# Warm-up matmuls on a constant, two more groups of them in the first step, and four score matmuls in another order

## The chip, the cores and the metric

The kernel runs on one core of one Trainium2 chip. The metric is device time of one execution in microseconds (us), as a median over runs. Less is better.

## What is computed

The reference chains three parts, all in float32:

```python
# attention: 2 batches x 8 heads, 768 tokens, head size 64
q_bucket = sum(((q @ proj) > 0) * 2**arange(6))     # six sign bits per query, the same for keys
mask     = q_bucket[..., :, None] == k_bucket[..., None, :]
scores   = where(mask, (q @ k.T) / sqrt(64), -1e9)
attn     = softmax(scores) @ v
x        = attn as (1536 tokens, 512)
# two feed-forward layers, 512 -> 2048 -> 512
h = x @ w_in;  g = h * sigmoid(1.702 * h);    x = g @ w_out
h = x @ w_in;  g = h * tanh(softplus(h));     out = g @ w_out
```

## The kernel before, in words

The kernel gets float32 precision out of float32r matmuls (one reduced-precision product each) by splitting operands into a high and a low part and adding three products. It has two stages: attention (about the first 226 us) and the feed-forward layers.

Attention is a pipeline of 96 steps, 16 heads with 6 blocks of 128 queries each. The order of every engine's instructions is written out by hand in the loop over `i` at the end of `attention` (the string `ORDER` and the table `todo`); the scheduler changes nothing, and each engine works through its own list in that order. In a step, `qk` (L512 to L526) computes one block of 128 x 768 scores in two PSUM halves of 384 columns: two matmuls of `qx` with `kh` (the scaled dot products) and then two of `qb` with `kb`, the sign bits and the rest of the split operands, which add the mask. Below, these second two are "the mask rows". `clamp` (L528, VectorE) takes the row minimum, `expo` (L537, ScalarE) the exponential, `trp` (L577) transposes on TensorE, `trl` (VectorE) makes the low part, and `pv` (L597) multiplies with the values. The score tile `s` has two buffers, so the scores of step 2 wait until the clamp of step 0 has read its tile.

Ahead of the loop stands what this change touches. `ident`, a 128 x 128 identity, is made on GpSimd, and TensorE then runs `NWARM` = 24 transposes of it into a PSUM tile nobody reads (L365 to L367). Meanwhile the first head's operands arrive and are prepared in `first` (L454 to L483): `qk_m`, `kh` and `qx` on VectorE and ScalarE, a copy into `qb` and one into `kb` on GpSimd (`pcopy`, L91), six matmuls `logits` (L425, tiles `pt`) for the sign bits, a comparison on VectorE (L479) that writes the bits into `qb`, and a copy of them into `kb` on ScalarE (L483). After that `qk(0)` is called once, and the loop calls `qk(1)` in its first step:

```python
            qk(0)
            for i in range(NSTEP + PVLAG):
...
                    elif op == "Q" and i + 1 < NSTEP:
                        qk(i + 1)
```

Of the kernel before, what the change touches and what calls it, by code (L numbers as in the profile page):

```python
# [12 lines left out]
F32 = mybir.dt.float32  # L13
# [27 lines left out]
def lsh_attention_moe_kernel(  # L41
# [10 lines left out]
    nc = tc.nc  # L52
    B, H, D, S = qt.shape
    NTOK, DM = out.shape
    P = 128
# [13 lines left out]
    NWARM = 24  # L69
# [222 lines left out]
    def r_in(m, f, k0=0, k1=KD):  # L292
        if k0 == 0:
            pool, tag = mps["h"], f"h{f % 2}"
            if (m, f // 2) == (0, 1):
                pool, tag = (mps["q"], "Y") if f % 2 else (mps["h"], "y0")
            h_t[m, f] = pool.tile([P, CH], F32, tag=tag, name="h")
        h = h_t[m, f]
        wh, wl = w_t[m, f, 0]
        n = 3 * k0  # L300
        for kk in range(k0, k1):
            wk = slice(kk * P, (kk + 1) * P)
            for a, x in ((wh, xr_hi), (wh, xr_lo), (wl, xr_hi)):
                nc.tensor.matmul(  # L304
                    h, a[:, wk], x[:, kk], start=(n == 0), stop=(n == 3 * KD - 1)
                )
                n += 1

    def attention():
        with ExitStack() as es:  # L310
# [7 lines left out]
            ps_t = es.enter_context(tc.tile_pool(name="ps_t", bufs=3, space=PSUM))  # L318
            ps_u = es.enter_context(tc.tile_pool(name="ps_u", bufs=1, space=PSUM))
            es_s = ExitStack()  # L320
            ps_s = es_s.enter_context(tc.tile_pool(name="ps_s", bufs=2, space=PSUM, side="right"))
# [40 lines left out]

            ident = cst.tile([P, P], F32, name="ident")
            make_identity(nc, ident)
            warm = ps_t.tile([P, 512], F32, tag="pt", name="warm")  # L365
            for _ in range(NWARM):
                nc.tensor.transpose(warm[:, :P], ident, ident)  # L367
            zero = pp.tile([P, 2, HS], F32, tag="p", name="zero").rearrange("p a b -> p (a b)")
            nc.vector.memset(zero[32:64], 0.0)
            qb_tiles = [cst.tile([P, S], F32R, name=f"qb{i}") for i in range(2)]  # L370
# [132 lines left out]
            st_t = {}  # L503
# [5 lines left out]
            rb_t = {}  # L509
            scr = dr.tile([NHD, S], F32, name="scr")  # L510

            def qk(i):  # L512
                n, t = divmod(i, NT)
                kh, qx, qb, kb, _ = opnd[n]
                s = ps_s.tile([P, 2, 512], F32, tag="s", name="s")
                c = slice(t * P, (t + 1) * P)
                for a, bb, st in ((qx, kh, True), (qb, kb, False)):
                    for f in range(2):
                        nc.tensor.matmul(  # L519
                            s[:, f, :HS],  # L520
                            a[:, c],
                            bb[:, f * HS : (f + 1) * HS],
                            start=st,
                            stop=not st,
                        )
                st_t[i] = s  # L526

            def clamp(i):  # L528
                s = st_t[i]
                sb = pp.tile([P, 2, HS], F32, tag="p", name="p")  # L530
                mn = sm.tile([P, 1], F32, tag="mn", name="mn")
                nc.vector.tensor_scalar(  # L532
                    sb, s[:, :, :HS], NEG, None, ALU.min, ALU.min, accum_out=mn
                )
                st_t[i] = (sb, mn)

            def expo(i):  # L537
                sb, mn = st_t.pop(i)
                n, t = divmod(i, NT)
                p = sb.rearrange("p a b -> p (a b)")  # L540
                if t == 0:
                    z_t[n] = sm.tile([P, NT], F32, tag="z", name="z", bufs=3)
                nc.scalar.activation(  # L543
                    p,
                    p,
                    AF.Exp,
                    bias=mn,
                    scale=-1.0,
                    accum_out=z_t[n][:, t : t + 1],
                )  # L550
                p_t[i] = p
# [25 lines left out]
            def trp(g, t):  # L577
                ptile = ps_t.tile([P, 512], F32, tag="pt", name="pt")
                for j in range(3):
                    nc.tensor.transpose(  # L580
                        ptile[:, j * P : (j + 1) * P],
                        p_t[3 * g + j][:, t * P : (t + 1) * P],
                        ident,
                    )
                hi = ptp.tile([P, HS], F32R, tag="pth", name="pth")
                lo = ptp.tile([P, HS], F32R, tag="ptl", name="ptl")
                nc.scalar.copy(hi, ptile[:, :HS])  # L587
                pt_t[g, t] = (hi, lo, ptile)

            def trl(g, t):  # L590
                hi, lo, ptile = pt_t[g, t]
                nc.vector.tensor_sub(lo, ptile[:, :HS], rnd(hi))  # L592
                if t == NT - 1:
                    for j in range(3):
                        p_t.pop(3 * g + j)

            def pv(g, t):  # L597
                n, f = divmod(g, 2)
                hi, lo, _ = pt_t.pop((g, t))
                if t == 0:  # L600
                    u_t[g] = ps_u.tile([P, 512], F32, tag="u", name="u")
                ut = u_t[g]
                vv = opnd[n][4][0]
                nc.tensor.matmul(ut[:, :HS], vv[:, t, :], hi, start=(t == 0), stop=False)  # L604
                nc.tensor.matmul(ut[:, :HS], vv[:, t, :], lo, start=False, stop=(t == NT - 1))  # L605
                if t == NT - 1:
                    u_out(g)
# [93 lines left out]
            for k in range(2):  # L701
                st = NSTEP - 4 * NT * (2 - k)
# [15 lines left out]
            for n, g in enumerate((ssums, ssums, ssums, ssums, ssplit, ssplit)):  # L718
                at(NSTEP - 12 + n, sgo, g, 0, 0)

            qk(0)
            for i in range(NSTEP + PVLAG):
                if i == NSTEP:
                    es_s.close()
                    mps["h"] = ctx.enter_context(
                        tc.tile_pool(name="ps_h", bufs=1, space=PSUM, side="right")
                    )
                parts = iter(range(max(0, 2 * (i - NSTEP)), min(2 * (i - NSTEP) + 2, 2 * KD)))
                for part in parts:
                    r_in(0, part // KD, part % KD, part % KD + 1)  # L730
                    break
                kk = i - LAG
                tr = 0 <= kk < NSTEP
                g, j = divmod(kk, 3)
                kv = i - PVLAG
                gv, jv = divmod(kv, 3)
                for op in ORDER:
                    if op == "A" and tr:
                        trp(g, 2 * j)
                    elif op == "B" and tr:  # L740
                        trp(g, 2 * j + 1)
                    elif op == "a" and tr:
                        trl(g, 2 * j)
                    elif op == "b" and tr:
                        trl(g, 2 * j + 1)
                    elif op == "C" and i < NSTEP:
                        clamp(i)
                    elif op == "E" and i < NSTEP:
                        expo(i)
                    elif op == "Q" and i + 1 < NSTEP:  # L750
                        qk(i + 1)
                    elif op == "P" and 0 <= kv < NSTEP:
                        pv(gv, 2 * jv)
                    elif op == "R" and 0 <= kv < NSTEP:
                        pv(gv, 2 * jv + 1)
                    elif op == "T":
                        while todo and min(todo) <= i:
                            st = min(todo)
                            f, args = todo[st].pop(0)
                            if not todo[st]:  # L760
                                del todo[st]
                            f(*args)
                for part in parts:
                    r_in(0, part // KD, part % KD, part % KD + 1)
# [5 lines left out]
    def moe():  # L770
        with ExitStack() as es:
# [266 lines left out]
            while due:  # L1038
                flush()

    attention()
    moe()

# [58 lines left out]
```

## Time and profile before

| | |
|---|---|
| median of 3 runs | 737.72 us (737.62 to 738.42) |
| the profiled execution's own time | 737.77 us |
| its span, first to last instruction | 736.0 us |
| TensorE busy | 728.4 us, 99% of the span |
| VectorE, ScalarE, GpSimd busy | 602.1, 423.8 and 186.0 us |

The rows come from one profiled execution. Times count from the start of its span. PE is TensorE's matmul, PEld its weight load, DVE VectorE, ACT ScalarE, POOL GpSimd, SP SyncE, and L12 is line 12 of the kernel. Matmuls are pipelined, so a matmul's own duration is longer than the distance from it to the next one. A releaser, after the arrow, is what ended an engine's idle time.

### The profile page before, as it was taken

The numbers are of one execution on the slowest core, as the hardware profiler recorded it, in microseconds if no ns is written. First come the engines' busy times: TensorE is split into PE (matmuls) and PEld (weight loads), VectorE is DVE, ScalarE is ACT, GpSimd is POOL, SyncE is SP. The second block draws the span as 40 slices with busy tenths as digits, with TensorE's granted clock in tenths as the row PEclk, the third lists the DMA queues.
The fourth block names the chain that finished last, engine by engine and source line by source line (L and its number), as shares of the span: only waits on it lengthen the run. The fifth ranks groups of instructions, "written<-read, shape, count | busy, mean of one in ns | idle before, by whom it ended". The sixth has DMA issues, their size and how long they took to land.

```text
span 736.0 us, 10689 instructions
## 1 busy us (share of the span) xinstructions
PE 728.4 (99%) x3694; PEld 631.8 (86%) x3694; DVE 602.1 (82%) x1100; ACT 423.8 (58%) x846; POOL 186.0 (25%) x190
## 2 busy tenths in 40 slices
PE   8999999999999999999999999999999999999997
PEld 7999999999998788888888888888888888888886
DVE  8888889989988958786687897997598797978854
ACT  7888888888888756426153461574555254352420
POOL 8868877887893000000000000000000000000000
PEclk9999999999999999999999999999999999999999
DMA  6665565566524312031221331101131211311004
GB/s 163 164 153 151 158 176 152 158 174 163 170 73 132 95 57 86 29 114 35 80 75 41 114 116 58 57 1 57 58 115 35 80 60 55 109 35 58 1 0 172
DMA packets 26054, 69.59 MB, mean 95 GB/s; under 512 B 4464, under 2 KB 6992, under 8 KB 26000
## 3 DMA queue, kind: packets, MB, share of 16 engines
q1 hardware_dynamic: 25712, 68.81, 31.5%
q8 instruction: 29, 0.48, 0.3%
q14 instruction: 25, 0.20, 0.1%
q10 hardware_dynamic: 288, 0.10, 0.1%
HBM read 49.19 MB, written 3.19 MB: 71 GB/s over the span
## 4 chain that ended last, share of the span: by engine, by line
PE 94%; ACT 3%; DMA 1%; DVE 1%; issue 1%; POOL 0%; ACTq 0%; POOLq 0%
PE y L835 36%; PE h L304 12%; PE X L889 9%; PE s L519 8%; PE pt L580 8%; PE Y L889 6%; PE W L889 6%; PE u L605 4%; PE u L604 4%; PE prep L425 2%; ACT p L543 2%; ACT pth L587 1%; DMA qn<-in_qt_dram 0%; DMA ul<-uh 0%; DVE p L532 0%
## 5 line engine op out<-in xcount | busy, mean ns | idle before, releaser
L592 DVE TENSOR_TENSOR ptl<-pt,pth 128x384 fp32r<-128x384 f32 x192 | 98.2, 553 | 25.3 <-ACT pth L587 24.6
L587 ACT CAST pth<-pt 128x384 fp32r<-128x384 f32 x192 | 83.0, 484 | 30.2 <-PE pt L580 30.0
L217 ACT CAST wh<-wb 128x512 fp32r<-128x512 f32 x64 | 39.7, 621 | 105.0 <-DVE wb L201 53.4
L849 DVE TENSOR_TENSOR xq<-xq,y 128x512 f32<-128x512 f32 (+1 forms) x113 | 76.6, 680 | 21.9 <-PE y L835 20.8
L543 ACT ACTIVATE p<-p,mn 128x768 f32<-128x768 f32 x96 | 91.1, 949 | 1.6 <-DVE p L532 1.5
L532 DVE TENSOR_SCALAR_CACHE_REDUCE p<-s 128x768 f32<-128x768 f32 x96 | 90.5, 944 | 0.4 <-PE s L519 0.4
L580 PE MATMUL pt<-ident,p 128*128 128x128 f32 x576 | 80.9, 274 | 0.6 <-ACT p L543 0.3
L835 PE MATMUL y<-wl,gh 128*128 128x512 f32 (+1 forms) x194 | 75.1, 387 | 0.0
L835 PE MATMUL y<-wh,gl 128*128 128x512 f32 (+1 forms) x194 | 75.1, 387 | 0.0
L835 PE MATMUL y<-wh,gh 128*128 128x512 f32 (+1 forms) x194 | 75.1, 387 | 0.0
L835 PE MATMUL y<-gh,wh 128*128 128x512 f32 x192 | 74.9, 390 | 0.0
L835 PE MATMUL y<-gl,wh 128*128 128x512 f32 x192 | 74.7, 389 | 0.0
L835 PE MATMUL y<-gh,wl 128*128 128x512 f32 x192 | 74.7, 389 | 0.0
L580 PEld LDWEIGHTS pt<-ident,p 128*128 128x128 f32 x576 | 68.3, 140 | 7.3 <-ACT p L543 2.0
L604 PE MATMUL u<-pth,vv 128*128 128x384 f32 x192 | 64.9, 338 | 0.0
L605 PE MATMUL u<-ptl,vv 128*128 128x384 f32 x192 | 64.8, 337 | 0.0
L519 PE MATMUL s<-kh,qx 128*128 128x384 f32 x192 | 55.4, 369 | 0.4 <-DVE p L532 0.4
L519 PE MATMUL s<-kb,qb 128*128 128x384 f32 x192 | 50.0, 340 | 0.6 <-POOL kb L91 0.5
L304 PE MATMUL h<-xr_hi,wh 128*128 128x512 f32 x128 | 50.0, 390 | 0.0
L304 PE MATMUL h<-xr_hi,wl 128*128 128x512 f32 x128 | 49.8, 389 | 0.0
L304 PE MATMUL h<-xr_lo,wh 128*128 128x512 f32 x128 | 49.8, 389 | 0.0
L219 DVE TENSOR_TENSOR wl<-wb,wh 128x512 fp32r<-128x512 f32 x62 | 42.5, 687 | 5.5 <-ACT wh L217 4.6
(202 smaller groups left out, 1678.1 us busy)
## 6 DMA issues: line engine op xcount, KB each, us to landing
raw<-in_wt_dram SPq DMA_DIRECT2D x64, 512.0 KB
kn<-in_kt_dram SPq DMA_DIRECT2D x15, 384.0 KB
qn<-in_qt_dram SPq DMA_DIRECT2D x16, 192.0 KB
vn<-in_vt_dram SPq DMA_DIRECT2D x8, 384.0 KB
ul<-uh SPq DMA_DIRECT2D x16, 192.0 KB
rb<-scr SPq DMA_DIRECT2D x16, 192.0 KB
qx<-qk_m SPq DMA_DIRECT2D x15, 192.0 KB
qb<-qk_m SPq DMA_DIRECT2D x15, 192.0 KB
```

The lines of the kernel that those rows point to most:

```text
L304: nc.tensor.matmul(h, a[:, wk], x[:, kk], start=(n == 0), stop=(n == 3 * KD - 1))
L519: nc.tensor.matmul(s[:, f, :HS], a[:, c], bb[:, f * HS : (f + 1) * HS], start=st, stop=not st,)
L532: nc.vector.tensor_scalar(sb, s[:, :, :HS], NEG, None, ALU.min, ALU.min, accum_out=mn)
L543: nc.scalar.activation(p, p, AF.Exp, bias=mn, scale=-1.0, accum_out=z_t[n][:, t : t + 1],)
L580: nc.tensor.transpose(ptile[:, j * P : (j + 1) * P], p_t[3 * g + j][:, t * P : (t + 1) * P], ident,)
L587: nc.scalar.copy(hi, ptile[:, :HS])
L592: nc.vector.tensor_sub(lo, ptile[:, :HS], rnd(hi))
L604: nc.tensor.matmul(ut[:, :HS], vv[:, t, :], hi, start=(t == 0), stop=False)
L605: nc.tensor.matmul(ut[:, :HS], vv[:, t, :], lo, start=False, stop=(t == NT - 1))
L835: nc.tensor.matmul(y, w[:, js] if m == 0 else x[:, js], x if m == 0 else w[:, i0:i1], start=(n == 0), stop=(n == 5),)
L849: nc.vector.tensor_add(acc, acc, y)
L889: nc.tensor.matmul(bk[b], w[:, k], x, start=(first and n == 0), stop=(hook is not None and n == 2), skip_group_check=True,)
```

## The change

The 24 warm-up instructions become plain float32 matmuls of a constant tile of ones (128 x 128 stationary, 64 moving columns) in place of transposes of `ident`. The same helper is called twice more, with 3 and with 6 matmuls. `qk` can now issue its two halves apart, and the first two matmuls of step 1 are issued ahead of the mask rows of step 0.

```diff
-            warm = ps_t.tile([P, 512], F32, tag="pt", name="warm")
-            for _ in range(NWARM):
-                nc.tensor.transpose(warm[:, :P], ident, ident)
+            ones = nc.const_aps.tensor(1.0, [P, P], F32)
+
+            def keep_warm(n):
+                t = ps_t.tile([P, 512], F32, tag="pt", name="warm")
+                for _ in range(n):
+                    nc.tensor.matmul(t[:, :64], ones, ones[:, :64], start=True, stop=True)
+
+            keep_warm(NWARM)
...
-            def qk(i):
+            def qk(i, parts=(0, 1)):
                 n, t = divmod(i, NT)
                 kh, qx, qb, kb, _ = opnd[n]
-                s = ps_s.tile([P, 2, 512], F32, tag="s", name="s")
+                if 0 in parts:
+                    st_t[i] = ps_s.tile([P, 2, 512], F32, tag="s", name="s")
+                s = st_t[i]
                 c = slice(t * P, (t + 1) * P)
-                for a, bb, st in ((qx, kh, True), (qb, kb, False)):
+                both = (qx, kh, True), (qb, kb, False)
+                for a, bb, st in [both[x] for x in parts]:
...
-            qk(0)
+            qk(0, (0,))
+            qk(1, (0,))
+            keep_warm(3)
+            qk(0, (1,))
...
-                        qk(i + 1)
+                        qk(i + 1, (0, 1) if i else (1,))
+                        if i == 0:
+                            keep_warm(6)
```

TensorE is the only engine whose list changes. Its list before, from the warm-up to the scores of step 2 (`s_208`, `s_222` and `s_236` are the score tiles of steps 0, 1 and 2):

```order
L367 MATMUL warm_128<-ident_123 128x128 x24
L425 MATMUL pt_193<-qk_m_170,pwt_164 128x384
...
L425 MATMUL pt_197<-qx_169,pwt_164 128x384
L519 MATMUL s_208<-kh_168,qx_169 128x384 x2
L519 MATMUL s_208<-kb0_157,qb0_155 128x384 x2
L519 MATMUL s_222<-kh_168,qx_169 128x384 x2
L519 MATMUL s_222<-kb0_157,qb0_155 128x384 x2
L519 MATMUL s_236<-kh_168,qx_169 128x384 x2
```

The same stretch of TensorE's list in the change (the score tiles of steps 0, 1 and 2 are `s_208`, `s_211` and `s_247` there, and the line numbers are those of the changed kernel):

```order
L372 MATMUL warm_128<-const-float32-1.0 128x64 x24
L432 MATMUL pt_193<-qk_m_170,pwt_164 128x384
...
L432 MATMUL pt_197<-qx_169,pwt_164 128x384
L529 MATMUL s_208<-kh_168,qx_169 128x384 x2
L529 MATMUL s_211<-kh_168,qx_169 128x384 x2
L372 MATMUL warm_214<-const-float32-1.0 128x64 x3
L529 MATMUL s_208<-kb0_157,qb0_155 128x384 x2
L529 MATMUL s_211<-kb0_157,qb0_155 128x384 x2
L372 MATMUL warm_231<-const-float32-1.0 128x64 x6
L529 MATMUL s_247<-kh_168,qx_169 128x384 x2
```

Between the two groups of `s_208` now stand the first two matmuls of step 1 and three warm-ups; six more warm-ups stand between step 1 and step 2. The lists of VectorE, ScalarE, GpSimd and SyncE hold the same instructions in the same order as before.

## Rows read from the trace of the kernel before

**Rows 1.** The page's parts 1 and 4: busy time by engine, and the chain that ended last.
```profile
PE 728.4 (99%) x3694; PEld 631.8 (86%) x3694; DVE 602.1 (82%) x1100; ACT 423.8 (58%) x846; POOL 186.0 (25%) x190
...
PE 94%; ACT 3%; DMA 1%; DVE 1%; issue 1%; POOL 0%; ACTq 0%; POOLq 0%
```

**Rows 2.** Busy time by stretch; after the engines the granted clock, DMA share and GB/s.
```profile
0.00:7.40 7.40, 6.02 (x26) 5.65 (x27) 5.59 (x8) 5.48 (x10) 4.57 (x12) 1.00 0.69 195
7.40:14.00 6.60, 5.68 (x30) 4.67 (x28) 5.61 (x11) 3.92 (x8) 6.30 (x6) 1.00 0.70 173
14.00:16.00 2.00, 1.86 (x15) 1.60 (x14) 1.76 (x4) 1.58 (x5) 1.83 (x3) 1.00 0.32 74
16.00:20.00 4.00, 4.00 (x28) 3.71 (x26) 4.00 (x10) 4.00 (x10) 3.83 (x4) 1.00 0.71 167
30.00:60.00 30.00, 30.00 (x203) 29.24 (x202) 26.48 (x59) 25.49 (x61) 20.56 (x21) 1.00 0.60 152
```

**Rows 3.** The chain of waits from 0 to 17 us, in order of time.
```profile
8.36 0.84 POOL kb L91
...
9.25 0.45 PE s L519
9.69 0.03 issue
9.73 0.46 PE s L519
10.19 0.02 issue
10.21 0.98 DVE p L532 x2
11.19 0.04 issue
11.23 0.98 PE s L519 x4
12.21 0.02 issue
12.23 0.98 DVE p L532 x2
```

**Rows 4.** Timeline, 0 to 20 us: start us, us, what, count, idle before.
```profile
0.95 0.70 DVE L369 MEMSET zero<- 32x768 f32 x1 [0.95 <-PEq L1082]
...
7.88 1.25 DVE L479 TENSOR_SCALAR qb<-pt,mc 64x384 fp32r<-64x384 f32 x2 [0.79 <-PE pt L425]
...
8.58 1.10 ACT L483 CAST kb<-qb 32x384 fp32r<-32x384 f32 x2 [1.00 <-DVE qb L479]
...
10.36 0.52 PE L519 MATMUL s<-kb,qb 128*128 128x384 f32 x2
...
11.10 0.95 DVE L532 TENSOR_SCALAR_CACHE_REDUCE p<-s 128x768 f32<-128x768 f32 x1
```

**Rows 5.** The tile of the warm-up: min/median/max ns, first and last start.
```profile
L367 PEld LDWEIGHTS warm<-ident x24: 183/230/230, 1.4 to 6.1; 128*128 128x128 f32 x24
L367 PE MATMUL warm<-ident x24: 421/421/476, 1.4 to 6.3; 128*128 128x128 f32 x24
```

**Rows 6.** TensorE's timeline in the steady pipeline.
```profile
35.59 0.82 PE L580 MATMUL pt<-ident,p 128*128 128x128 f32 x6
```

**Rows 7.** Groups by shape: count, then busy us, mean ns, idle before and its releasers.
```profile
L580 PE MATMUL pt<-ident,p 128*128 128x128 f32 x576 | 80.9, 274 | 0.6 <-ACT p L543 0.3
```

**Rows 8.** TensorE's timeline: start us, us, what, count, idle before and its releaser.
```profile
1.36 5.38 PE L367 MATMUL warm<-ident 128*128 128x128 f32 x24 [1.36 <-POOL ident masks.py:199]
6.76 0.66 PE L425 MATMUL pt<-qk_m,pwt 128*128 128x384 f32 x1
7.22 0.44 PE L425 MATMUL pt<-kh,pwt 128*128 128x384 f32 x1
7.50 0.33 PE L425 MATMUL pt<-qx,pwt 128*128 128x384 f32 x1
7.68 0.33 PE L425 MATMUL pt<-qk_m,pwt 128*128 128x384 f32 x1
...
8.20 0.51 PE L519 MATMUL s<-kh,qx 128*128 128x384 f32 x2
```

**Rows 9.** Line L465, which writes the operand of the first `logits` matmul.
```profile
L465 DVE TENSOR_TENSOR qk_m<-kn,kh x2: 542/806/1071, 5.5 to 6.5; 64x384 fp32r<-64x384 f32 x2
```

**Rows 10.** Weight loads by shape: two products with the same weights, in a later stage.
```profile
L835 PEld LDWEIGHTS y<-wh,gl 128*128 128x128 f32 x194 | 36.4, 188 | 7.4
...
L835 PEld LDWEIGHTS y<-wh,gh 128*128 128x128 f32 x194 | 36.4, 188 | 7.4
```

**Rows 11.** TensorE's waits for weights, 0 to 30 us: engine, line, releaser, total, times, longest.
```profile
PEld s L519 <- POOL kb L91: 0.9, 1, 0.9
PEld s L519 <- DVE p L532: 0.7, 1, 0.7
```

More of the change, by code (lines that the diff above doesn't have):

```diff
@@ L525, in qk @@
                         )
-                st_t[i] = s
             def clamp(i):
```

## The prediction, as made before the changed kernel was run

> **What bounds the kernel now.** I read the page first, then the busy time by stretch, then the timeline and the chain of the first 17 us, because the change touches nothing later. TensorE is busy 99% of the span and carries 94% of the chain that ended last [rows 1]. From 16 us on there is no room left: it is busy 4.00 of 4.00 us, and later 30.00 of 30.00 [rows 2]. So whatever the start gains or loses is carried to the end unchanged, and the forecast is one sum: by how much the scores of step 2 move, which are the last thing that still waits in the start.
>
> In the first 14 us TensorE is not yet the bound. The chain there reads [rows 3]: GpSimd's copy into `kb` ends at 9.20, the mask rows of step 0 start at 9.25 (first half) and 9.73 (second half), the clamp of step 0 at 10.21, the scores of step 2 at 11.23 once that clamp has given the tile back, the clamp of step 2 at 12.23. The second half waits for ScalarE's copies into `kb` (8.58, 1.10 us for two), and these for VectorE's comparison at 7.88, and that for the `logits` matmuls [rows 4].
>
> **The clock.** The granted-clock column shows 1.00 from the first stretch on [rows 2], but the durations say otherwise, and I go by them. The 24 transposes start from 1.4 to 6.3 us, 4.9/23 = 0.213 us apart [rows 5]. The same instruction later comes every (0.82 - 0.27)/5 = 0.11 us (six in 0.82, of which the last one's duration is 0.27) [rows 6, 7]. 128 columns loaded and 128 streamed, one after the other, are 256 columns: 0.213 us at 1.2 GHz, 0.107 at 2.4. So the warm-up runs at the low level throughout. The first `logits` matmul takes 0.66 us, the second 0.44, all from 7.50 on 0.33 [rows 8]: the clock rose between 7.2 and 7.5, say 7.44, 6.1 us after TensorE began at 1.36.
>
> **Removed: the wait for `ident`.** TensorE waited until 1.36 for GpSimd's identity [rows 8]. VectorE, free of that, starts at 0.95 [rows 4], and so will the warm-up: 0.41 us earlier. By itself this is worth nothing, because the first `logits` matmul is not held by the warm-up. Its operand comes from VectorE's L465, which starts at 5.5 and takes 1.07, so ends at 6.6 [rows 9], and the matmul starts at 6.76. It can bring a clock that rises earlier. With the clock up, the three `logits` of the first half lie 0.17 us apart, as at 7.50 and 7.68, and the last starts at 7.10 rather than 7.50 [rows 8]: up to 0.35 us for the chain. There it stops, since GpSimd's 9.20 then ends last.
>
> **Added: 24 float32 matmuls of 64 columns for 24 transposes.** No such instruction is in the trace. All others here are float32r or transposes, so its price is the unknown of this forecast. Bounds from the nearest rows, at the low clock: below, one load of 128 and one stream of 64 columns, 192 columns or 0.16 us; above, four products (high and low of both operands), each with its own load, 4 x 192 = 768 columns or 0.64 us. That loads aren't shared is what a later stage shows: L835 multiplies with `wh` twice, and each of the two products has its 194 loads [rows 10]. I take the middle: two loads (a high and a low stationary operand) and four streams, 512 columns, 0.427 us at the low and 0.213 at the full clock. It is nearest to the transposes' row, at twice its price. The Trainium skill, "TensorE: Matmul & The Clock Gate", section "Terms", says that the transpose mode is 4 times faster for FP32. By that page a plain matmul of half as many columns would cost two transposes, an estimate of 0.427 us too; no run yet shows it.
>
> The sum: TensorE starts at 0.95 and the clock rises 6.1 us later, at about 7.03. By then 6.08/0.427 = 14.2 are done, and the other 9.8 take 9.8 x 0.213 = 2.1 us. The warm-up ends at 9.1, and the first `logits` starts there instead of 6.76. The warm-up has become a wait. From there the old distances hold, at the full clock: the third `logits` ends 0.68 after the first starts and VectorE begins 0.04 later; from its start at 7.88 to the second half of the mask rows at 9.73 it was 1.85 us [rows 3, 4]. So the mask rows' second half is at 9.1 + 0.72 + 1.85 = 11.7, against 9.73.
>
> **Moved: two matmuls of step 1, and 3 warm-ups.** On TensorE's own list, six `logits` and four score matmuls at 0.175 (7.50 to 8.20 is four of them [rows 8]) and three warm-ups at 0.213 put the first half of the mask rows at 9.1 + 1.75 + 0.64 = 11.5 and the second at 11.65. This lies just beside the chain's 11.7, so it costs nothing here. The move itself gains nothing: step 1's mask rows were done by 10.88, and VectorE came to that tile at 11.10, straight from the clamp of step 0 [rows 4].
>
> **Added: 6 warm-ups ahead of step 2.** TensorE's wait for the first clamp had 0.7 us [rows 11]. Counted from the second half of the mask rows, the scores of step 2 came 11.23 - 9.73 = 1.50 us later. Now three more matmuls (0.52) and six warm-ups (1.28) must pass: 1.80. That is 0.30 over the old wait. At 0.107 each they would fit into it.
>
> **Sum.** Scores of step 2 at 11.7 + 1.8 = 13.5 instead of 11.23: +2.25 us. The profiled execution took 737.77 us, which is 0.05 over the median of the runs, so the forecast is **740.0 us**. Its own range: with the clock rising at 7.44 as before, the warm-up ends 0.2 later, 740.2 or 740.3. At the other end stands a rule: the Trainium skill, same page, section "Part 4: PE-mode transpose", says that transposes don't count as activity for the clock. The trace neither proves nor excludes it: the clock rose 0.7 us after the first real matmul, and 6.1 us after the first transpose. As a mechanism of this kernel: the clock rises 0.7 us after the first real matmul, now at about 1.65 us; 1.6 of the warm-ups are done by then, and the other 22.4 end at 6.4, ahead of 6.76. Then the first term gains 0.35, the six warm-ups cost 0.30, and the time is 737.7. By that rule the sum would be no change.
>
> **Rivals.** About 0.2%, 1.5 us, is what a measurement of this kernel can tell from no change.
>
> *A, the warm-up stays cover* (not slower): a plain float32 matmul costs about what a transpose does, 0.213 or less. 24 of them end at 0.95 + 5.1 = 6.06, before the operands at 6.6; six at 0.107 take 0.64 and fit into the 0.98 that the wait leaves (1.50 - 0.52). What is left is nothing up to the 0.35 us of an earlier clock: 737.4 to 737.8. For it: the same data type and the same weight columns as the transposes. Against: high precision is not for nothing on this engine, since the kernel itself buys it with three products each. It decides below about 0.3 us each.
>
> *B, four full passes* (much slower): 0.64 and 0.32. At 7.03, 9.5 are done, and 14.5 take 4.6: the warm-up ends at 11.7. TensorE's own list now orders the mask rows: 1.75 + 0.96 + 0.17 = 2.9 later, 14.6; then 0.52 + 6 x 0.32 = 2.44: step 2 at 17.0, +5.7, 743.5 (743 to 744 with the clock's rise). For it: the unshared loads of L835 [rows 10].
>
> *C, the clock comes late*: if the warm-ups are so short (0.16 us) that they end at 4.8, TensorE idles for 1.9 us up to 6.76, and the clock could stay low through the start. The TensorE pieces of the chain from 9.25 to 12.21 (0.45, 0.46, 0.98) [rows 3] would double: +1.9, 739.7. Against it: the clock held through waits of 0.9 and 0.7 us [rows 11].
>
> A gain of over 1.5 us has no source: beyond the 0.35 us everything in the chain belongs to a transfer, GpSimd or VectorE, which the change leaves alone.
>
> **How the numbers follow.** Forecast 0.40, A 0.34, B 0.22, C 0.04. The forecast falls past 1.5 us with three quarters of its chance, 0.30, and with 0.22 of B and 0.03 of C slower has 0.55; A and the rest make 0.42 for no change; 0.03 for faster by something that I don't see. A and B lie on either side, so the range takes in both: 737.3 to 743.8, where the forecast's own is 737.7 to 740.3.
>
> **What would show it.** The distance of one warm-up to the next at the low clock: 0.43 for the forecast, 0.21 or less for A, 0.64 for B. The start of the first `logits` matmul: 9.1, 6.7, 11.7. Step 2's scores: 13.5, about 11, 17. The durations of `logits` show the clock at that time. I am wrong if the `logits` start at 6.8 or before and the time still changes by over 1.5 us, or if TensorE after 20 us is not as full as before.

## The result, and the profile after

| | before | after |
|---|---|---|
| median of 5 runs each | 737.72 us (737.54 to 738.42) | 744.32 us (743.83 to 745.26) |
| the profiled execution | 737.77 us, span 736.0 | 743.98 us, span 742.2 |

The ratio is 1.009, with a 95% interval of 1.0075 to 1.0105: slower by 6.6 us. The forecast of 740.0 had the sign and not the size, and the time lies 0.5 us over the upper end of the range.

The page after, its span and its part 1, against [rows 1]: TensorE has 7.5 us more work, the other engines about what they had.

```profile
span 742.2 us, 10773 instructions
...
PE 735.9 (99%) x3736; PEld 640.2 (86%) x3736; DVE 603.6 (81%) x1100; ACT 424.5 (57%) x846; POOL 186.4 (25%) x190
```

TensorE's timeline after, from its first instruction to the scores of step 2 (start, us, what, count, idle before), against [rows 8]:

```profile
0.77 10.47 PE L372 MATMUL warm<-const-float32-1.0 128*128 128x64 f32 x48 [0.77 <-PEq L1096]
11.00 0.67 PE L432 MATMUL pt<-qk_m,pwt 128*128 128x384 f32 x1
...
11.79 0.52 PE L432 MATMUL pt<-qx,pwt 128*128 128x384 f32 x1
...
12.75 0.52 PE L432 MATMUL pt<-qx,pwt 128*128 128x384 f32 x1
13.07 1.32 PE L529 MATMUL s<-kh,qx 128*128 128x384 f32 x4
14.23 0.78 PE L372 MATMUL warm<-const-float32-1.0 128*128 128x64 f32 x6
14.82 0.94 PE L529 MATMUL s<-kb,qb 128*128 128x384 f32 x4
15.60 1.45 PE L372 MATMUL warm<-const-float32-1.0 128*128 128x64 f32 x12
16.86 0.59 PE L529 MATMUL s<-kh,qx 128*128 128x384 f32 x2
```

Three things are to be seen. Each float32 matmul of ones stands in the trace as two pairs of a weight load and a matmul: 48 for 24, 6 for 3, 12 for 6. The 48 pairs end at 11.0, so one pair takes (11.00 - 0.77)/48 = 0.213 us and one matmul 0.426. And the `logits` behind them still come 0.32 us apart with 0.52 each, where they were 0.18 apart with 0.33 [rows 8]: the clock is at its low level. The six pairs from 14.23 come 0.1 us apart, (14.82 - 14.23)/6, so it rose at about 14.

The chain of waits after, 0 to 20 us, against [rows 3]: GpSimd's `kb` and the first clamps are gone from it. From 0.77 to 17.81 TensorE waits for nothing but itself.

```profile
0.77 10.47 PE warm L372 x48
11.24 2.03 PE pt L432 x6
13.27 1.12 PE s L529 x4
14.39 0.61 PE warm L372 x6
15.01 0.75 PE s L529 x4
15.76 1.28 PE warm L372 x12
17.05 0.77 PE s L529 x4
```

The wait has changed sides: VectorE, which TensorE waited for at the first `logits`, now waits for the `logits` (waits, 0 to 24 us, in total, times, longest).

```profile
DVE qb L486 <- PE pt L432: 5.6, 2, 5.3
```

Busy time after by stretch, against [rows 2]: from 30 to 60 us TensorE is as full as before.

```profile
30.00:60.00 30.00, 30.00 (x202) 29.26 (x200) 26.64 (x58) 24.81 (x58) 19.75 (x20) 1.00 0.55 142
```

Step 2's scores stand at 16.86 against 11.23, +5.63; the span grew by 6.2. The other 0.55 are lost at 204 us, where VectorE's L201, which prepares weights between two clamps, takes 1.62 us in place of 0.68. The timeline, first before, then after; of it two instructions of GpSimd and VectorE's L201:

```profile
184.81 0.83 POOL L406 TENSOR_SCALAR qk_m<-qn 64x768 fp32r<-64x768 f32 x1
...
195.16 1.29 POOL L636 TENSOR_TENSOR xq<-ul,rb 128x512 f32<-128x512 f32 x1
...
197.07 0.68 DVE L201 SCALAR_TENSOR_TENSOR wb<-wb,raw 128x512 uint32<-128x512 uint32 x1
```

```profile
192.13 0.83 POOL L413 TENSOR_SCALAR qk_m<-qn 64x768 fp32r<-64x768 f32 x1 [1.75 <-DMA qn<-in_qt_dram]
...
202.47 1.27 POOL L645 TENSOR_TENSOR xq<-ul,rb 128x512 f32<-128x512 f32 x1
...
202.68 1.62 DVE L201 SCALAR_TENSOR_TENSOR wb<-wb,raw 128x512 uint32<-128x512 uint32 x1
```

Before, GpSimd's instruction had ended (196.45) when L201 began. Now it began 0.21 us ahead of L201 and ended at 203.74, and L201 ended 0.56 after that, at 204.30. The Trainium skill, "SBUF — State Buffer", section "SBUF: two separate sides", says that GpSimd and a VectorE instruction with two SBUF inputs, as L201 is, lock a shared pair of ports for a whole instruction and that the second fully blocks; the two rows agree with it to about 0.1 us (203.74 and L201's old 0.68 make 204.42).

An equal shift of all engines would not have brought the two together. L201 came 5.61 us later than before, GpSimd's instruction 7.31, because GpSimd waited 1.75 us ahead of 192.13 for the load of a later head's queries. Before, at 184.81, it had not waited for that load.

### The profile page after: what moved, and what is told of

Same layout as the page of the kernel before. It is cut to its first block, busy times and chain, and to the rows that moved or that the text cites. A ratio compares the mean times of both kernels' runs of the same rounds, so it can differ in the third digit from the quotient of the medians.

```text
span 742.2 us, 10773 instructions
## 1 busy us (share of the span) xinstructions
PE 735.9 (99%) x3736; PEld 640.2 (86%) x3736; DVE 603.6 (81%) x1100; ACT 424.5 (57%) x846; POOL 186.4 (25%) x190
## 4 chain that ended last, share of the span: by engine, by line
PE 94%; ACT 3%; DVE 1%; issue 1%; DMA 0%; ACTq 0%
PE y L849 35%; PE h L304 12%; PE X L903 9%; PE s L529 8%; PE pt L589 8%; PE Y L903 6%; PE W L903 6%; PE u L614 4%; PE u L613 4%; PE prep L432 2%; PE warm L372 2%; ACT p L552 2%; ACT pth L596 1%; DMA ul<-uh 0%; DVE wb L201 0%
```

## The experiments

Theory T: a float32 matmul costs 0.427 us at the low clock, and the 64-column matmuls do not raise the clock, so the warm-up is 10.25 us long and all up to about 14 us runs at the low level. Rival R1: the loss belongs to the extra groups and the new order, not to the first warm-up. Rival R2: it is not the width, but that they are ones, or float32, or no transposes. An interval in brackets is that of the ratio to the kernel before, run on the same chip beside it. The kernel before itself had medians of 738.85 (chip of the first four), 737.81 (next four) and 737.69 (last three).

**e1: half as long.** Against the changed kernel:

```diff
-    NWARM = 24
+    NWARM = 12
```

> The change with 12 ones-matmuls at the start in place of 24; the rest of the change stays. Theory (the loss is the length of the first warm-up: 0.427 us each at the low clock, and these narrow matmuls do not raise the clock): the 12 end at 0.77 + 12 x 0.427 = 5.9 us, the first logits matmul starts with its operand at 6.7 to 6.8, the logits lie 0.32 us apart because the clock is still low, the scores of step 2 start at 11.3 to 12.5, and the time is 737.7 to 739.0 us. Rival (the extra warm-ups and the order in the first step are what costs): the time stays over 742 us.

Measured: 739.89 (739.18 to 740.75, 10 runs), 1.0016 [1.0004, 1.0028]. Of its TensorE timeline:

```profile
0.77 5.35 PE L372 MATMUL warm<-const-float32-1.0 128*128 128x64 f32 x24 [0.77 <-PEq L1096]
...
7.51 0.52 PE L432 MATMUL pt<-qx,pwt 128*128 128x384 f32 x1
...
10.07 1.38 PE L372 MATMUL warm<-const-float32-1.0 128*128 128x64 f32 x6
...
13.98 0.59 PE L529 MATMUL s<-kh,qx 128*128 128x384 f32 x2
```

The `logits` start at 6.73 again, as before the change: the warm-up no longer stands in their way, and about 4.4 us of the loss are gone. But it came out 0.9 over my 739.0. I had the clock rise too soon: the `logits` are at the low level (0.52), so is the group of three (1.38 in place of 0.78), and it rose only at about 12.8. 5 us of these matmuls had not helped. Step 2's scores, expected by 12.5, came at 13.98.

**e2: the change with the old warm-up**, new order and both extra groups kept. Against the changed kernel:

```diff
-            keep_warm(NWARM)
+            warm = ps_t.tile([P, 512], F32, tag="pt", name="warm")
+            for _ in range(NWARM):
+                nc.tensor.transpose(warm[:, :P], ident, ident)
```

> The change with the 24 transposes of the identity of before as the first warm-up; the order and the groups of 3 and 6 ones-matmuls stay. Theory (length of the first warm-up): the logits start at 6.7 to 6.8 as before, the groups of 3 and 6 at the full clock cost at most 0.5 us (6 x 0.224 = 1.34 us against the 0.98 us that the wait leaves), so 737.6 to 738.4 us. Rival (extra warm-ups and order cost): over 742 us.

Measured: 738.35 (737.92 to 742.36, 10 runs), 1.0002 [0.9986, 1.0017]: the loss is gone, so R1 falls. The warm-up's tile (min, median, max ns, first and last start), then TensorE's timeline:

```profile
L376 PE MATMUL warm<-ident x24: 272/421/472, 1.4 to 6.1; 128*128 128x128 f32 x24
L372 PE MATMUL warm<-const-float32-1.0 x18: 218/275/275, 8.6 to 11.3; 128*128 128x64 f32 x18
```

```profile
6.74 0.42 PE L434 MATMUL pt<-qk_m,pwt 128*128 128x384 f32 x1 [0.41 <-DVE qk_m L474]
...
9.32 0.96 PE L531 MATMUL s<-kb,qb 128*128 128x384 f32 x4
10.12 1.45 PE L372 MATMUL warm<-const-float32-1.0 128*128 128x64 f32 x12
11.38 0.59 PE L531 MATMUL s<-kh,qx 128*128 128x384 f32 x2
```

The last transposes take 272 ns against the 421 of most, and all had started by 6.1, before the first matmul at 6.74. So here the clock rose while nothing but transposes had run. The extra six also show their price at the full clock: the second half of the mask rows is at 9.60, step 2 at 11.38, 1.78 later, where it was 1.50 before. That is +0.28.

**e3: only the warm-up changed**; the order of before, no extra groups. Against the changed kernel:

```diff
-            qk(0, (0,))
-            qk(1, (0,))
-            keep_warm(3)
-            qk(0, (1,))
+            qk(0)
...
-                        qk(i + 1, (0, 1) if i else (1,))
-                        if i == 0:
-                            keep_warm(6)
+                        qk(i + 1)
```

> Only the first warm-up of the change (24 ones-matmuls); the order of before and no groups of 3 and 6. Theory (length of the first warm-up): the logits start at 11.0, the clock is low through them, and the time is 743.0 to 744.3 us, at most 1 us below the change. Rival (extra warm-ups and order cost): 737.3 to 738.0 us.

Measured: 743.37 (742.92 to 743.92, 4 runs), 1.006 [1.0041, 1.0079]. TensorE's timeline:

```profile
11.01 0.67 PE L432 MATMUL pt<-qk_m,pwt 128*128 128x384 f32 x1
...
16.19 0.61 PE L529 MATMUL s<-kh,qx 128*128 128x384 f32 x2 [0.48 <-DVE p L541]
```

The warm-up alone is nearly the whole loss: step 2 at 16.19, +4.96. Order and extras make the other 0.67, up to 16.86. Behind step 2 this execution loses another 0.6 us, about as much as after does at 204: TensorE waits 0.3 us at 24 us for a mask transfer, and L201 once takes 1.39 us beside GpSimd (at 147.67).

**e4: three wide ones for 24 narrow.** Against the changed kernel; the extra groups stay as they are:

```diff
-            ones = nc.const_aps.tensor(1.0, [P, P], F32)
+            ones = nc.const_aps.tensor(1.0, [P, 512], F32)
...
-            def keep_warm(n):
+            def keep_warm(n, w=64):
...
-                    nc.tensor.matmul(t[:, :64], ones, ones[:, :64], start=True, stop=True)
+                    nc.tensor.matmul(t[:, :w], ones[:, :P], ones[:, :w], start=True, stop=True)
...
-            keep_warm(NWARM)
+            keep_warm(3, 512)
```

> The change with 3 ones-matmuls of 512 columns at the start in place of 24 of 64; the rest stays. Each should take 2 x 1024 columns at 1.2 GHz or about 1.7 us, so they end near 5.9 us. Theory a (the narrow shape is why the clock stayed low): the clock rises before 8 us, the logits from the second or third on lie 0.17 us apart, the time is 737.3 to 738.3 us. Theory b (constant data or this data type cannot raise the clock): the logits lie 0.32 us apart and the time is as with 12 narrow ones, 737.9 to 739 us.

Measured: 738.99 (737.80 to 739.74, 10 runs), 0.9997 [0.9986, 1.0009]. TensorE, then GpSimd:

```profile
0.77 5.46 PE L372 MATMUL warm<-const-float32-1.0 128*128 128x512 f32 x6 [0.77 <-PEq L1096]
6.76 0.41 PE L432 MATMUL pt<-qk_m,pwt 128*128 128x384 f32 x1 [0.53 <-DVE qk_m L472]
...
11.01 0.96 PE L529 MATMUL s<-kb,qb 128*128 128x384 f32 x4 [1.63 <-POOL kb L91]
```

```profile
8.45 0.83 POOL L413 TENSOR_SCALAR qk_m<-qn 64x768 fp32r<-64x768 f32 x1 [2.23 <-DMA qn<-in_qt_dram]
```

The same ones in the same data type raise the clock: the first `logits` take 0.41 and lie 0.17 to 0.19 apart. Ones, float32 and the lack of transposes are out of R2. The time is still 0.7 us over theory a, and what this execution loses is another thing. GpSimd's copy into `kb` stands behind its work on the second head's queries (`q1()` in `first`), and this waited 2.23 us for their load, where before it waited 1.24; the mask rows come at 11.01. That needed runs of its own (e7, e8, e10).

**e5: the wide warm-up alone, in the kernel before.**

```diff
+            ones = nc.const_aps.tensor(1.0, [P, 512], F32)
...
-            for _ in range(NWARM):
-                nc.tensor.transpose(warm[:, :P], ident, ident)
+            for _ in range(3):
+                nc.tensor.matmul(warm, ones[:, :P], ones, start=True, stop=True)
```

> The kernel before with its 24 transposes replaced by 3 ones-matmuls of 512 columns; the order of before, no extra groups. Theory (wide matmuls raise the clock as the transposes do, and earlier, since TensorE starts at 0.77 instead of 1.36): the logits lie 0.17 to 0.18 us apart from the first or second on, the scores of step 2 start 0 to 0.4 us before those of before with equal landing of the second head's queries, and the time is within 0.4 us of before, not above it. Rival (only transposes bring a steady rise; the wide case was luck): logits 0.32 us apart and 1 to 2.5 us over before.

Measured: 737.65 (737.45 to 740.47, 10 runs), 1.0004 [0.9990, 1.0018]; step 2 at 11.06 in the profiled execution. Three wide matmuls do what 24 transposes did, and no more.

**e6: almost no warm-up.** Against the kernel before:

```diff
-            for _ in range(NWARM):
-                nc.tensor.transpose(warm[:, :P], ident, ident)
+            nc.tensor.transpose(warm[:, :P], ident, ident)
```

> The kernel before with 1 warm-up transpose in place of 24. Theory (the narrow ones-matmuls do as little for the clock as no warm-up at all): as in the run with 12 narrow ones, the first logits start at 6.7, the logits lie 0.32 us apart, the clock rises after 9 us, and the time is 1 to 2.5 us over before. Rival (the clock rises a fixed time after TensorE's first instruction or the program's start, whatever it does): the logits lie 0.17 us apart from 7.5 us on and the time is that of before within 0.3 us.

Measured: 740.12 (738.81 to 740.85, 10 runs), 1.0018 [1.0005, 1.0031]. TensorE's timeline:

```profile
6.80 0.66 PE L424 MATMUL pt<-qk_m,pwt 128*128 128x384 f32 x1 [4.97 <-DVE qk_m L464]
7.26 0.52 PE L424 MATMUL pt<-kh,pwt 128*128 128x384 f32 x1
...
13.03 0.62 PE L518 MATMUL s<-kh,qx 128*128 128x384 f32 x2 [0.77 <-DVE p L531]
```

Without a warm-up the `logits` look as in e1, 0.66 and then 0.52. Against e1's 739.89 it is the same time: for the clock, twelve narrow matmuls are worth as little as none.

**e7: the wide warm-up, and GpSimd's copy into `kb` first.** Against the kernel before, e5's edit and this one:

```diff
+                    pcopy(kb[D:P], rnd(qk_m[D:P]))
                     q1()
-                    pcopy(kb[D:P], rnd(qk_m[D:P]))
```

> The kernel before with the 3 wide ones-matmuls as warm-up, and GpSimd's copy into the first head's kb ahead of its work on the second head's queries, which waits for their transfer. Theory (with the clock up, GpSimd's copy at 9.2 us ends last, and it ends late because it stands behind a wait for a transfer): the copy ends at about 8 us, the second half of the mask rows starts at 9.3 to 9.5, step 2's scores at 10.7 to 11.0, and the time is 0.2 to 0.6 us below before where that transfer lands early and up to 2 us below where it lands late. Rival (GpSimd's later work on the second head then ends last): no gain against the wide warm-up alone.

Measured: 737.44 (737.25 to 737.84, 10 runs), 0.9984 [0.9973, 0.9994]. GpSimd's timeline:

```profile
7.13 0.83 POOL L91 TENSOR_SCALAR kb<-qk_m 64x768 fp32r<-64x768 f32 x1 [0.95 <-DVE qk_m L466]
```

The copy ends at 7.96 instead of 9.20 [rows 3], step 2 comes at 10.91, and of ten runs none is over 737.84.

**e8: the kernel before, unchanged, a second profile.**

> The kernel before, for a second trace of it. Theory (the second head's queries land at different times, which moves GpSimd's copy into kb, and the clock rises at a different time from run to run): a span of 735.7 to 736.2 us with the landing near 7.4 us and the clock up by 7.5, or 737 to 738.7 us with the landing after 8.4 us or the clock up later. Either is possible.

Measured: one run of 739.67, near the upper end of its own spread. GpSimd's timeline, then TensorE's:

```profile
8.85 0.82 POOL L406 TENSOR_SCALAR qk_m<-qn 64x768 fp32r<-64x768 f32 x1 [2.61 <-DMA qn<-in_qt_dram]
9.75 1.60 POOL L91 TENSOR_SCALAR kb<-qk_m 64x768 fp32r<-64x768 f32 x1
```

```profile
11.41 0.62 PE L519 MATMUL s<-kb,qb 128*128 128x384 f32 x2 [2.87 <-POOL kb L91]
```

The times of the kernel before spread from 737.4 to 740.4, and this run shows what e4 showed: GpSimd had the second head's queries at 8.85 instead of 7.45, and the copy, which now falls beside a VectorE instruction, took 1.60 instead of 0.83. 22 of the 68 runs of before in the three sets were over 739 (one of 4189 us is left out). The five runs of before beside the change all lie at 738.42 or below, so the loss of 6.6 us is counted from the lower end; from the medians of the three sets it would be 5.5 to 6.6.

**e9: only the new order**, in the kernel before (transposes, no extra groups; `qk` can be issued by halves, as in the change):

```diff
-            qk(0)
+            qk(0, (0,))
+            qk(1, (0,))
+            qk(0, (1,))
...
-                        qk(i + 1)
+                        qk(i + 1, (0, 1) if i else (1,))
```

> The kernel before with only the new order of the four score matmuls (step 1's first two ahead of step 0's mask rows), no ones-matmuls anywhere. Theory (VectorE comes to step 1's tile straight from the clamp of step 0, so earlier scores of step 1 gain nothing, and the wait ahead of the mask rows hides the two moved matmuls): step 2's scores start 1.4 to 1.6 us after the second half of the mask rows, as before, and the time is that of before within 0.3 us at equal landing of the second head's queries. Rival (the move saves TensorE work in the first step): step 2's scores at least 0.2 us earlier against the mask rows.

Measured: 738.55 (737.34 to 740.42, 10 runs), 1.0003 [0.9988, 1.0019]: no gain and no loss that these runs can tell. The five runs under 739, without the late landing as far as the time tells, have a median of 737.55, the 14 of before beside them 737.61. The profiled execution (739.38) has the late landing; step 2's scores start 1.45 us after the second half of the mask rows (12.23 - 10.78), as expected. Its busy time by stretch (TensorE, its loads, VectorE, ScalarE, GpSimd, granted clock, DMA share, GB/s):

```profile
7.00:10.94 3.94, 2.19 (x12) 1.88 (x12) 2.27 (x4) 1.86 (x3) 2.92 (x3) 1.00 0.38 100
10.94:14.35 3.41, 2.99 (x11) 2.48 (x10) 2.28 (x5) 1.95 (x4) 3.24 (x4) 0.50 0.94 273
```

TensorE was busy 2.19 of 3.94 us, with 1.75 us in one wait for `kb`, and then the clock fell back to 0.50 (1.2 GHz) for 3.4 us. It is not the wait's length alone: in e8 the clock stayed up through one of 2.87 us. The mean granted clock of every run is on record, and it tells how common this is: it was 0.998 in this execution, and 0.998 or less in 19 of the 22 runs of before over 739, but in only 1 of its 46 others. So most of the upper end is a late load with a fall of the clock; e8, at 1.000, had the late load alone.

Extra matmuls in that wait are what the change might have been good for. e4, which has them, had 5 of 10 runs over 739, all with 0.999 or more. e5 with the same warm-up and no extras had 4 and e9 with the order alone had 5, all with 0.998 or less. But e2, which has the extras too, had 2 of 10 over 739, and the slower (742.36) had 0.995. So the runs speak for it and do not show it.

One more row of this execution bears on the clock, the tile of its warm-up:

```profile
L376 PE MATMUL warm<-ident x24: 272/381/477, 1.4 to 5.2; 128*128 128x128 f32 x24
```

The first of the same 24 transposes starts at 1.4 as before, the last at 5.2 and not at 6.3 [rows 5]: here the clock rose in the middle of them.

**e10: only the copy into `kb` first**, in the kernel before, with its transposes: e7's swap of two lines and nothing else.

> The kernel before with only GpSimd's copy into kb put ahead of its work on the second head's queries; warm-up transposes as before. Theory (the wait for that transfer, ahead of the copy, is what spreads the times of before from 737.4 to 740.2 us): no run over 738.5 us, median 737.3 to 737.9 us, the copy starting at about 7.1 us. Rival (the wide warm-up is what narrowed the times of the kernel that had both): times up to 740 us as before.

Measured: 737.46 (737.36 to 737.72, 10 runs), 0.9988 [0.9977, 0.9998], step 2 at 10.90. The swap alone gives what e7 gave; the wide warm-up is not needed for it. Together with e7 that is 20 runs without one over 737.84 and without one whose granted clock is below 0.999. So it is the wait for the late load, ahead of the copy, that set the spread, with the fall of the clock that often came behind it.

**e11: width alone.** e5's edit with eight matmuls of 128 columns in place of three of 512:

```diff
+            for _ in range(8):
+                nc.tensor.matmul(warm[:, :P], ones[:, :P], ones[:, :P], start=True, stop=True)
```

> The kernel before with 8 ones-matmuls of 128 columns as warm-up. If a load of 128 and twice 128 streamed columns add up in each of two passes, each takes 2 x 384 columns at 1.2 GHz, 0.64 us, and they end near 5.9 us. Theory (columns streamed against columns loaded make the difference between the 64- and the 512-column matmuls): the clock rises before 8 us, as with the transposes, and the logits come to lie 0.17 us apart. Rival (only the widest matmuls do it): logits 0.32 us apart through all six.

Measured: one run of 737.41. The warm-up's tile, then TensorE's timeline:

```profile
L368 PE MATMUL warm<-const-float32-1.0 x16: 421/421/551, 0.8 to 4.1; 128*128 128x128 f32 x16
```

```profile
0.77 3.75 PE L368 MATMUL warm<-const-float32-1.0 128*128 128x128 f32 x16 [0.77 <-PEq L1083]
6.79 0.41 PE L426 MATMUL pt<-qk_m,pwt 128*128 128x384 f32 x1 [2.26 <-DVE qk_m L466]
```

My price was wrong: I expected 0.32 us for a pair, and it takes (4.1 - 0.8)/15 = 0.22, the pace of 64 columns. That made the run a sharper test than planned. Same operand, data type, weights and pace; 16 pairs of 128 columns have the clock up by 6.79, and 48 pairs of 64 columns had not by 11.0. Only the width is different, and the count, which speaks for the narrow ones. R2 falls.

**What the start is worth at the end.** Step 2's scores and the span in the 13 profiled executions:

| | scores of step 2, us | span, us | difference |
|---|---|---|---|
| before, e8 | 11.23, 13.09 | 736.0, 737.9 | 724.8, 724.8 |
| after | 16.86 | 742.2 | 725.3 |
| e1, e2 | 13.98, 11.38 | 738.9, 736.1 | 724.9, 724.7 |
| e3 | 16.19 | 741.6 | 725.4 |
| e4, e5, e6 | 13.07, 11.06, 13.03 | 737.7, 735.8, 737.7 | 724.6, 724.7, 724.7 |
| e7, e10, e11 | 10.91, 10.90, 10.95 | 735.6 each | 724.7, 724.7, 724.7 |
| e9 | 12.23 | 737.6 | 725.4 |

Ten lie within 0.3 us of each other. e9 goes on at the low clock after its step 2. The other two are after and e3, and they are the only ones in which an instruction of L201 took over 0.72 us. The line L201 (min, median, max ns) in after, then in e3; in before its longest is 719. The 1649 of after is a second one, at 233.0 us:

```profile
L201 DVE SCALAR_TENSOR_TENSOR wb<-wb,raw x38: 681/686/1649, 148.0 to 469.6; 128x512 uint32<-128x512 uint32 x38
```

```profile
L201 DVE SCALAR_TENSOR_TENSOR wb<-wb,raw x38: 681/685/1394, 147.7 to 468.9; 128x512 uint32<-128x512 uint32 x38
```

## Why the prediction was wrong, point by point

- **The start.** "0.41 us earlier" was 0.59: TensorE starts at 0.77, ahead of VectorE's 0.95. It changed nothing of weight.
- **The price of a float32 matmul: right, in part by luck.** 0.427 us at the low clock and 0.213 at the full one were forecast; 0.426 and 0.21 (e2's twelve pairs in 1.26 us) were measured. Rival A fell with it, and so did B: its 743.5 us lies near the result, but its 0.64 us for each matmul is not what happened.
- **Its make-up: not right.** The sum behind the price, two loads and four streams one after the other, does not hold: it gives 768 columns or 0.64 us for 128 moving columns, where e11 measured 0.43, what 64 cost. At 512 columns a pair comes every 0.853 us (e4: from the second at 1.76 to the sixth at 5.17), which is 1024 columns at 1.2 GHz: an estimate of two streams of 512 in each pair, with no time left for the load. The estimate of two transposes for half the columns met the number too, but not its factor of 4: at 128 columns the matmul costs two transposes. And [rows 10] do not show what they were taken for: the second name is the loaded operand, so `y<-wh,gl` and `y<-wh,gh` have different weights. The two that share theirs, `y<-wh,gh` and `y<-wl,gh`, have 194 loads each as well, so the reading stands on them.
- **The clock: here it failed.** The step is "TensorE starts at 0.95 and the clock rises 6.1 us later, at about 7.03". I took one event of the trace of before, the rise 6.1 us after the first instruction, for a clock that runs from TensorE's start whatever TensorE does. With 64-column matmuls it did not rise in the 10.2 us of the warm-up at all; it rose at about 14, some 3 us after the first `logits`, which e6 shows to be work that raises it by itself. So none of the 24 ran at half price, and the warm-up ended at 11.0 instead of 9.1. Nor are 6.1 us fixed for the transposes: the granted clock's record in the trace begins, at full speed, at 7.44 us before, and behind the same 24 transposes at 7.00 in e8, 6.02 in e10, 5.77 in e2 and 4.11 in e9, that is 2.8 to 6.1 us after their start.
- **The rule that was weighed.** The rival of no change (737.7) rested on a clock that only real matmuls raise. e2 refutes the reason: there it rose under transposes alone. The Trainium skill, "TensorE: Matmul & The Clock Gate", section "Part 4: PE-mode transpose", says that transposes don't count; here they did. The same page, "What's actually happening" in Part 1, says that a warm-up is a matter of time and not of the number of matmuls; after 10.2 us without a gap between the pairs the `logits` still ran at the low level, and here the measurement decides.
- **"From there the old distances hold, at the full clock"** fell with it. At the low clock `logits` and first scores were a further 0.72 us for the chain (e3: 4.96 - 4.24), and in the change the chain lay on TensorE's own list, not on VectorE, ScalarE and GpSimd.
- **The move of two matmuls: right.** Nothing gained, nothing lost (e9: step 2 follows the mask rows by 1.45 us, as by 1.50 before, and 737.55 against 737.61 over the runs under 739).
- **The extra groups: right in size.** +0.30 was forecast for the six; +0.28 in e2, and 0.67 with the new order at the mixed clock of the change.
- **"Whatever the start gains or loses is carried to the end unchanged"**: nearly. The table shows it to 0.3 us in ten executions. In after and e3 an instruction of VectorE met one of GpSimd. In after it was not the shift itself that brought them together but a load, for which GpSimd waited 1.75 us where it had not waited before; in e3 GpSimd's instruction came 5.93 us later than before (147.50 against 141.57) and VectorE's 5.25, behind a wait of GpSimd for such a load of 1.87 us where before it was 1.18. That is read from the two engines' rows; no kernel was made that keeps them apart.

The sum again, with what was measured in the profiled executions, the terms in the middle as differences of runs: +4.24 for the warm-up's length (11.00 - 6.76), +0.72 for the low clock behind it, +0.67 for extras and order, +0.55 for the late meeting, 6.18 of the 6.2 us.

What stays open: why 64 columns don't raise the clock, of which only the fact is shown (the run with 128 columns is a single one); why the clock fell in e9 and not in e8; and whether the two extra groups keep it up through a late transfer.

## What to carry to other kernels

A warm-up has two properties, how long it is and whether it raises the clock, and both are read from the instruction used: look at the durations of the first real matmuls behind it, not at how busy TensorE was. Take for it an instruction that the trace has shown to do it (here transposes of 128 columns, or float32 matmuls of 128 or 512), and let it end before the first operand arrives. And look at which load an engine's in-order list waits for ahead of the work that the start needs: two swapped lines (e10: 737.46 us, 0.9988 [0.9977, 0.9998]) gained a little and took a spread of 3 us away, more than any warm-up did.

## What the runs showed of the hardware that I had not expected

- A float32 matmul is two pairs of load and matmul, 0.213 us a pair at the low clock for 64 and for 128 columns alike (after, e11), and 0.853 for 512 (e4).
- 48 pairs of 64 columns over 10.2 us left the clock at its low level; 16 pairs of 128 columns over 3.8 us, and 6 of 512 over 5.5 us, had it up by the first `logits` at 6.8 (e11, e4).
- The same 24 transposes had the clock up at 7.4 us in one execution and at 4.1 in another (before, e9).
- After a wait of 1.75 us, in a stretch with TensorE busy 2.19 of 3.94 us, the granted clock was 0.50 for 3.4 us (e9); after one of 2.87 us the matmuls ran at full speed (e8).
- The same load landed for GpSimd at 7.45 in one execution of the same kernel and at 8.85 in another (before, e8), and the later one met a VectorE instruction that stretched the copy from 0.83 to 1.60 us.
